# Attention weights turned by 32x32 blocks on VectorE and a DRAM scratch instead of on TensorE, in 22 of 32 attention units

## The chip, the cores and the metric

One core of a Trainium2 chip runs the whole program. The metric is device time in microseconds (us): the median of three runs of the kernel before is 690.51, with a lowest of 689.42 and a highest of 690.60. The engines are called PE (TensorE), DVE (VectorE), ACT (ScalarE), POOL (GpSimd) and SP (SyncE, which here only issues DMAs).

## What is computed

A sparse causal attention, then a two-layer block with the activation h·cos(h), all in float32 (4 batches, 8 heads, 768 positions, head size 64; 3072 tokens, model width 512, inner width 2048):

```python
scores = scale * np.matmul(q, k.transpose(0, 1, 3, 2))
keep = is_global | is_local            # first 8 keys, or the last 96 up to the query
scores = np.where(keep, scores + bias, -1000000000.0)
a = np.exp(scores - max); a = a / (sum + 1e-09)
x = np.matmul(a, v)                    # then heads side by side: tokens x 512
h = x @ w_in
out = (h * np.cos(h)) @ w_out
```

## The kernel before, in words

**Tiling.** Queries go in tiles of 96 (R). A tile sees its own 96 keys, the 96 before them and 8 global keys, so each tile keeps one row of 104 weights per query (SLOT): a column of the first 96 holds either an own key or, right of the diagonal, one of the 96 before (they never both count), and the last 8 columns are the global keys. Four tiles make a chunk of 384 tokens (8 chunks); two heads make a pair (4 pairs). A chunk and a pair make a *unit*: 32 units, numbered chunk by chunk.

**A unit** (`plan_unit`, then `plan_values`): scores on PE (L561; L557 in the first units), the fold of the two key blocks and the minimum on DVE (L574, L583), the exponential on ACT (L603), the normalization on POOL (`norm`, L631 or L626), one operation for each half of the unit (two tiles by two heads: 96 partitions x 4 x 104). Then the weights have to stand with keys on partitions: for each half `turn` (L693) does four PE transposes into a PSUM bank, and DVE writes the bank twice into the tile `pv`, through a mask, `others` (L701) for the keys of the block before and the globals, and `own` (L706) for the tile's own keys. In the leading tile of a sequence a plain copy (`whole`, L281) stands in for a mask. `av` (L728) multiplies by the values, 32 small matmuls (28 in a leading unit), and `high` (L281) and `rest` (L749) split the result into the two operands `xh`, `xl` of the next stage.

**The block.** A *step* is 128 of the 2048 inner columns for one chunk: 12 matmuls of 384 columns (`moe1`, L765), the activation on ACT and DVE (L782, L785, L788, L825), a split by `gh` (L285, L281 or L283) and `gl` (L838), and 9 matmuls of 512 columns (`moe2`, L776). There are 128 steps. `plan_store` writes finished rows out by way of the tiles `oo` (L281, L877), in two slots `wu`, in the last chunk in three slots `part`.

**The order.** A list scheduler written into the kernel (`Plan`) fixes the order of every engine before anything runs. Each operation has engines with a duration in ns, and a due time that is passed back from what needs it (`dues`); at each moment an engine takes the ready operation with the earliest due. So the engines' queues are in the order that the planner's own figures give. For an SP operation the figures are, in `run`:

```python
if e == SP:
    dma = max(end + 300, dma) + o.extra
    self.free[SP] = max(end, dma - DEPTH)
    end = dma + 1400
```

Here `end` is the issue's end (470 ns for every DMA of the kernel before), `extra` the time of the bytes, and 1400 the rest until others may go on. An operation marked `port=True` is kept from running on DVE while POOL runs, and the next POOL instruction is made to wait for it (`emit`). Buffers are slots by name: 5 of `tt` (weights, before they are turned), 3 of `pv`, 2 of `wu`, 3 of `part` (partial sums of chunk 0 while chunk 1 runs), 3 of `raw` (queries and keys as loaded), 3 PSUM banks for attention.

Of the kernel before, what the change touches and what calls it, by code (L numbers as in the profile page):

```python
# [10 lines left out]
F32 = mybir.dt.float32  # L11
# [7 lines left out]
ALU = mybir.AluOpType  # L19
PSUM = bass.MemoryType.PSUM  # L20

P = 128
# [3 lines left out]
G = 8  # L26
R = 96
SLOT = R + G
# [40 lines left out]

EXACT = 8  # L70

HOMES = 7

HOLD = 8
# [4 lines left out]
class Slot:  # L79


    def __init__(self, cls, make):
        self.cls, self.make = cls, make
        self.users = 0
        self.at = None
        self._tile = None
# [6 lines left out]


class Op:
    def __init__(self, engines, emit, after, uses, due, table, extra, port, mode):
        self.engines, self.emit, self.uses, self.due, self.table = engines, emit, uses, due, table
        self.extra, self.port, self.mode = extra, port, mode
        self.after = [a for a in after if a is not None]
        self.then = []  # L100
        self.left = len(self.after)
        self.ready = 0
        self.start = None


class Plan:
# [16 lines left out]
        self.port = self.hand = 0  # L123
        self.mode = None

    def op(self, engines, emit, after=(), uses=(), due=None, table=None, extra=0, port=False, mode=None):
        o = Op(engines, emit, after, list(uses), due, table, extra, port, mode)
        for a in o.after:
            a.then.append(o)
        for u in o.uses:  # L130
            u.users += 1
        self.ops.append(o)
        return o

    def dues(self):
        late = 10**9
        for o in reversed(self.ops):
            d = late if o.due is None else o.due
            for t in o.then:
                d = min(d, t.due - min(t.engines.values()) - self.WAIT[next(iter(o.engines))] - o.extra)  # L140
            o.due = d

    def place(self, u, t):
# [117 lines left out]
class Net:  # L261
# [376 lines left out]
    def plan_split(self, raw, src, k0, sc):  # L638
# [34 lines left out]
        k = p.op({DVE: 70 + w * 535 // 512, POOL: 100 + w * 1125 // 512}, krest, [k], [raw, kk], port=True)  # L673
        return [qq, kk], [q, k]

    def plan_values(self, u):
        nc, p, D = self.nc, self.plan, self.D
        n, pr, hs, vs, tt = u["n"], u["pr"], u["hs"], u["v"], u["tt"]
        att = "early" if n == 0 else "att"
        px = self.bank("pxearly" if n == 0 else "px")  # L680
        pvs, ready = [], list(u["lv"])
        for h in range(0, CT, 2):
            pt = self.bank(att)

            pv = Slot(self.early("pv", n, pr), lambda i: self.work.tile([P, 2, 4 * R], F32, name="pv", tag=i))
            lead = u["first"] and h == 0

            def turn(e, pt=pt, h=h, lead=lead):
                for t in range(2):
                    w = R if lead and t == 0 else SLOT  # L690
                    for j in range(2):
                        o = (2 * t + j) * R
                        nc.tensor.transpose(pt.tile[:w, o : o + R], tt[h // 2].tile[:, t, j, :w], self.ident[:R, :R])  # L693

            a = 2 if lead else 0

            wide = lambda x, a: x.rearrange("p (c i) -> p c i", i=R)[:, a:]
            mask = lambda m, a: m.rearrange("p (o i) -> p o i", o=1).broadcast_to([m.shape[0], 4 - a, R])

            def others(e, pt=pt, pv=pv, a=a):  # L700
                nc.vector.tensor_tensor(  # L701
                    wide(pv.tile[:SLOT, 0], a), wide(pt.tile[:SLOT, : 4 * R], a), mask(self.others, a), op=ALU.mult
                )

            def own(e, pt=pt, pv=pv, a=a):
                nc.vector.tensor_tensor(  # L706
                    wide(pv.tile[:R, 1], a), wide(pt.tile[:R, : 4 * R], a), mask(self.own, a), op=ALU.mult
                )

            def whole(e, pt=pt, pv=pv):  # L710
                self.copy(e, pv.tile[:R, 1, : 2 * R], pt.tile[:R, : 2 * R])

            o = self.chain("pt", p.op({PE: 340}, turn, [u["norm"][h // 2]], [pt, pv, tt[h // 2]]))
            d = 70 + (4 - a) * R * 104 // 100
            ready += [p.op({DVE: d}, fn, [o], [pt, pv]) for fn in (others, own)]
            if lead:
                ready.append(p.op({ACT: 50 + 2 * R * 427 // 512, DVE: 70 + 2 * R * 104 // 100}, whole, [o], [pt, pv]))
            pvs.append(pv)

        def av(e):  # L720
            for t in range(CT):
                pv = pvs[t // 2].tile
                lead = u["first"] and t == 0
                for c in (1,) if lead else (0, 1):
                    k = R if c else SLOT
                    for j in range(2):
                        o = (2 * (t % 2) + j) * R
                        nc.tensor.matmul(  # L728
                            px.tile[j * D : (j + 1) * D, t * R : (t + 1) * R],
                            vs.tile[:k, t + c, hs][:, j * D : (j + 1) * D],  # L730
                            pv[:k, c, o : o + R],
                            start=c == 0 or lead,
                            stop=c == 1,
                        )

        o = self.chain("av", p.op(
            {PE: 160 * (2 * CT - u["first"])}, av, ready, [px, vs] + pvs, mode="columns"))
        if n not in self.x:
            self.x[n] = Slot("x", lambda i: [
                self.work.tile([P, self.NP, CW], F32R, name=nm, tag=f"{nm}{i}") for nm in ("xh", "xl")  # L740
            ])
        x = self.x[n]

        def high(e):
            self.copy(e, x.tile[0][:, pr, :], px.tile[:, :CW])

        def rest(e):
            xh, xl = x.tile
            nc.vector.tensor_tensor(xl[:, pr, :], px.tile[:, :CW], xh.bitcast(F32)[:, pr, :], op=ALU.subtract)  # L749

        o = self.chain("xh", p.op({ACT: 370, DVE: 470}, high, [o], [px, x]))
        self.xdone[n, pr] = p.op({DVE: 470}, rest, [o], [px, x], due=self.xdue(n, pr))
# [264 lines left out]
    def run(self):  # L1017
        with ExitStack() as ctx:
            pool = lambda name, **kw: ctx.enter_context(self.tc.tile_pool(name=name, bufs=1, **kw))
            self.work, self.psum = pool("work"), pool("psum", space=PSUM)  # L1020
            with self.tc.manual_schedule():
                flag = self.windows()
        rv = self.nc.values_load(flag, min_val=0, max_val=P)
        with self.tc.If(rv > 0):
            self.general()

    def windows(self):

        NCK = self.B * self.NCH
        names = lambda nm, n: [f"{nm}{i}" for i in range(n)]  # L1030
        banks = names("b", 8)
        self.plan = Plan(
            {
                "ph": banks[0:2], "po0": banks[2:3], "po1": banks[3:4], "po2": banks[4:5], "att": banks[5:8],
                "px": banks[6:8], "early": banks[5:8] + banks[0:5], "pxearly": banks[6:8] + banks[2:5],
                "tt": names("tt", NT), "st": names("st", NST), "q": names("q", NQK), "k": names("k", NQK), "raw": names("raw", NRAW),
                "v": names("v", NV), "pv": names("pv", NPV), "ttearly": names("tt", NT) + names("k", 2),
                "vearly": names("v", NV) + ["q0"], "pvearly": names("pv", NPV) + ["q1"], "x": names("x", NX),
                "rr": names("rr", NRR), "gg": names("gg", NG), "wu": names("wu", 2), "part": names("part", NTOK),
            },  # L1040
            {PE: 400, ACT: 2400, DVE: 700, POOL: 5200, SP: 600},
        )
        self.prev, self.x, self.xdone, self.wdone, self.part = {}, {}, {}, {}, {}
        p = self.plan
        self.constants()
        self.tmp_slots = [Slot("tt", None) for _ in range(3)]
        self.plan_masks()
        phases = PHASES + [(n, 0, self.NF) for n in range(1 + max([x[0] for x in PHASES], default=-1), NCK)]
        self.seq = [(n, i, a, b - 1) for n, a, b in phases for i in range(a, b)]
        for n in range(NCK):  # L1050
            for b2 in range(self.NP // UB):
                L = self.plan_loads(n, b2)
                for i in range(UB):
                    self.plan_values(self.plan_unit(L, b2 * UB + i))
# [95 lines left out]
```

## Time and profile before

| | |
|---|---|
| timed runs | 689.42, 690.51, 690.60 us (median 690.51) |
| span of the profiled execution | 688.2 us, first to last instruction |
| its own time | not among the times shown; the timed runs lie 1.2 to 2.4 us over this span |
| PE busy | 674.0 us, 98% of the span |
| DVE, ACT, POOL busy | 417.9, 416.3, 332.7 us |
| DMA | 55.95 MB, mean 81 GB/s |
| granted TensorE clock, mean | 0.997 |

Matmuls are pipelined, so the busy time of one (246 ns for a transpose) is not what it adds to the queue; the chain of waits shows the distance from one to the next. An engine's idle time is shown with the event that ended it.

### The profile page before, as it was taken

To read this page: it belongs to the slowest core of one execution; us is meant where nothing else is said; L and a number is where in the kernel's file an instruction comes from. 1 tells how busy PE (TensorE), PEld (TensorE's weight loads), DVE (VectorE), ACT (ScalarE), POOL (GpSimd) and SP (SyncE) were. 2 spreads that over 40 slices of the span, in tenths; PEclk is the share of its full clock that TensorE was granted. 3 is DMA by queue.
4 is the path that set the end of the run, shared out by engine and by line. 5 is a ranking of instruction groups with operands and counts; after the bars stand their busy time and mean duration, and the time that the engine had idled before them with its cause. 6 is when DMAs were issued, how large, how long until landed. Compare 5 with 4: busy or idle time off the path is not lost.

```text
span 688.2 us, 12961 instructions
## 1 busy us (share of the span) xinstructions
PE 674.0 (98%) x4462; PEld 591.2 (86%) x4462; DVE 417.9 (61%) x1313; ACT 416.3 (60%) x1064; POOL 332.7 (48%) x427
## 2 busy tenths in 40 slices
PE   7999999999999999999999999999999999999995
PEld 4668899888898888888898888988889899898994
DVE  7998889976537665466736667266663566522221
ACT  6999987776546664665627666275663756423222
POOL 5777643435445553554534555345453455333332
PEclk9999999999999999999999999999999999999998
DMA  8899501142203222032322313032220310001001
GB/s 275 297 371 310 124 1 48 41 126 61 61 1 106 67 70 70 25 97 64 73 66 72 98 51 85 21 113 57 70 74 12 116 29 1 1 1 47 0 2 51
DMA packets 32603, 55.95 MB, mean 81 GB/s; under 512 B 3472, under 2 KB 18192, under 8 KB 32528
## 3 DMA queue, kind: packets, MB, share of 16 engines
q1 hardware_dynamic: 32528, 55.03, 27.2%
q8 instruction: 37, 0.61, 0.4%
q14 instruction: 38, 0.31, 0.2%
HBM read 48.73 MB, written 6.29 MB: 80 GB/s over the span
## 4 chain that ended last, share of the span: by engine, by line
PE 85%; ACT 6%; POOL 3%; DMA 2%; issue 2%; DVE 2%; SPq 0%; POOLq 0%; ACTq 0%
PE bank L776 37%; PE bank L765 36%; PE bank L728 5%; PE bank L561 5%; PE bank L693 2%; ACT tt L603 2%; DMA raw<-in_w_out_dram 1%; POOL ks L661 1%; POOL tt L631 1%; DMA out_dram<-oo 1%; DMA raw<-in_qk_dram 1%; POOL gl L838 1%; ACT L788 1%; DVE tt L583 0%; ACT w L281 0%
## 5 line engine op out<-in xcount | busy, mean ns | idle before, releaser
L765 PE MATMUL bank<-xh,w 128*128 128x384 f32 x1024 | 299.3, 342 | 1.0 <-DVE gl L838 0.8
L776 PE MATMUL bank<-w,gh 128*128 128x512 f32 x768 | 244.2, 399 | 0.0
L765 PEld LDWEIGHTS bank<-xh,w 128*128 128x128 f32 x1024 | 188.2, 188 | 9.5 <-DVE gl L838 1.8
L765 PE MATMUL bank<-xl,w 128*128 128x384 f32 x512 | 172.3, 336 | 0.0
L776 PEld LDWEIGHTS bank<-w,gh 128*128 128x128 f32 x768 | 137.9, 188 | 19.6 <-ACT tt L603 0.3
L776 PE MATMUL bank<-w,gl 128*128 128x512 f32 x384 | 151.4, 394 | 0.0
L285 POOL TENSOR_SCALAR gh<-rr 128x384 fp32r<-128x384 f32 x91 | 46.8, 514 | 210.4 <-PE bank L776 151.4
L785 DVE SCALAR_TENSOR_TENSOR rr<-rr,bank 128x384 f32<-128x384 int32 x129 | 70.5, 548 | 111.2 <-ACT rr L782 110.7
L782 ACT ACTIVATE rr<-bank 128x384 int32<-128x384 f32 x129 | 62.3, 484 | 116.4 <-PE bank L765 116.2
L788 ACT ACTIVATE rr<-rr,half_pi 128x384 f32<-128x384 f32 x129 | 79.0, 615 | 70.0 <-DVE rr L785 69.5
L765 PEld LDWEIGHTS bank<-xl,w 128*128 128x128 f32 x512 | 96.4, 188 | 4.0
L603 ACT ACTIVATE tt<-tt,worst 96x104 f32<-96x104 f32 (+1 forms) x256 | 94.4, 370 | 6.6 <-DVE worst L583 5.7
L838 POOL TENSOR_TENSOR gl<-rr,gh 128x384 fp32r<-128x384 f32 (+1 forms) x93 | 93.6, 1007 | 8.5 <-PE bank L693 1.5
L825 DVE TENSOR_TENSOR rr<-bank,rr 128x384 f32<-128x384 f32 (+1 forms) x121 | 66.2, 549 | 43.0 <-ACT rr L788 42.7
L776 PEld LDWEIGHTS bank<-w,gl 128*128 128x128 f32 x384 | 72.3, 188 | 16.7
L631 POOL TENSOR_TENSOR tt<-tt,st 96x416 f32<-96x416 f32 x48 | 42.3, 885 | 34.5 <-DVE qs L652 20.7
L583 DVE CUSTOM_DVE_ANT_0 tt<-bank,dd 96x104 f32<-96x104 f32 (+1 forms) x256 | 55.7, 257 | 2.6
L661 POOL TENSOR_TENSOR ks<-raw,ks 64x512 fp32r<-64x512 f32 (+1 forms) x39 | 47.9, 1227 | 5.4 <-POOL gl L838 2.5
L561 PEld LDWEIGHTS bank<-ks,qs 128*96 128x96 f32 x384 | 46.2, 162 | 4.6
L728 PEld LDWEIGHTS bank<-pv,v 104*64 104x64 f32 (+1 forms) x960 | 41.0, 136 | 9.2 <-issue 7.0
L561 PE MATMUL bank<-ks,qs 128*96 128x200 f32 (+1 forms) x384 | 48.2, 255 | 0.0
L603 ACT ACTIVATION_READ_ACCUMULATOR tt<-tt,worst 96x1 f32 x256 | 48.0, 188 | 0.0
(98 smaller groups left out, 730.2 us busy)
## 6 DMA issues: line engine op xcount, KB each, us to landing
raw<-in_qk_dram SPq DMA_DIRECT2D x64, 224.0 KB
raw<-in_w_out_dram SPq DMA_DIRECT2D x16, 512.0 KB
raw<-in_w_in_dram SPq DMA_DIRECT2D x16, 512.0 KB
raw<-in_qk_dram SPq DMA_DIRECT2D x32, 198.0 KB
out_dram<-oo SPq DMA_DIRECT2D x24, 256.0 KB
v<-in_v_dram SPq DMA_DIRECT2D x16, 240.0 KB
raw<-in_qk_dram SPq DMA_DIRECT2D x8, 396.0 KB
v<-in_v_dram SPq DMA_DIRECT2D x16, 192.0 KB
```

Source lines behind the costliest of these rows:

```text
L561: nc.tensor.matmul(out, qs[:, m, q0], ks[:, k : k + w], start=m == 0, stop=m == 1)
L583: nc.vector.tensor_tensor_reduce(tt[t // 2].tile[:, t % 2, j, :w], ps.tile[:R, i * WIN : i * WIN + w], self.dd[:, v, :w], op0=ALU.add, op1 ...
L603: nc.scalar.activation(x, x, AF.Exp, bias=lows[:, c : c + 1], scale=-1.0, accum_out=st.tile[:, c : c + 1])
L661: self.eng(e).tensor_tensor(ks[D:, k0:], raw.tile[D:, k0:KW], ks.bitcast(F32)[D:, k0:], op=ALU.subtract)
L728: nc.tensor.matmul(px.tile[j * D : (j + 1) * D, t * R : (t + 1) * R], vs.tile[:k, t + c, hs][:, j * D : (j + 1) * D], pv[:k, c, o : o + R] ...
L765: self.nc.tensor.matmul(ph[:, :CW], self.wi[f][:, w, kk * P : (kk + 1) * P], xx[:, kk, :], start=kk == 0 and m == 0, stop=kk == self.NK - ...
L776: self.nc.tensor.matmul(po, gg[:, ts], self.wo[f][:, w, :], start=start and m == 0, stop=stop and m == 2)
L782: self.nc.scalar.activation(r.bitcast(I32), ph, AF.Copy, scale=1.0 / TWO_PI, bias=0.25)
L785: self.nc.vector.scalar_tensor_tensor(r, r.bitcast(I32), -TWO_PI, ph, op0=ALU.mult, op1=ALU.add)
L788: self.nc.scalar.activation(r, r, AF.Sin, bias=self.half_pi)
L825: {DVE: dve}, lambda e, r=r, h=h, y=y: nc.vector.tensor_tensor(y(), h(), r(), op=ALU.mult), [o], [ph, rr]
L838: self.eng(e).tensor_tensor(g[1][:, cs], y(), g[0].bitcast(F32)[:, cs], op=ALU.subtract)
```

## The change

From unit 10 on (`TURN`), thus in 22 of the 32 units, `plan_moved` takes the place of the PE transposes. The earlier ten units keep the old way (`plan_turned`, the old code unchanged). For each half of a unit `plan_moved` does this:

- `turn` and `ends`, two DVE transposes by 32x32 blocks, out of `tt` into a tile `sw`: the first 96 columns of each row, and the last 32 columns, which hold the 8 global keys. `sw` uses the five slots `wu` and `part`.
- `store`, one DMA of `sw` (96 partitions x 2048 B) to a DRAM scratch `away` (six slots).
- three DMAs `move` back from it, each to 32 partitions in runs of 512 B, and `glob`, one for the 8 global rows; all wait for the store.
- `others` and `own` as before, but SBUF to SBUF, on POOL or DVE as the planner chooses.

`av` then reads each tile's weights as three runs of 32 columns, 128 apart. The number of matmuls in it is as before. The planner counts the landing of a DMA with 2000 ns more (`LAND`) when it passes back due times.

```diff
+TURN = 10
+LAND = 2000
+CB = R // 32
...
-                d = min(d, t.due - min(t.engines.values()) - self.WAIT[next(iter(o.engines))] - o.extra)
+                d = min(d, t.due - min(t.engines.values()) - self.WAIT[next(iter(o.engines))] - o.extra - o.land)
...
+    def plan_moved(self, u, h):
...
+        sw = Slot("sw", lambda i: self.work.tile([R, CB + 1, 4, 32], F32, name="sw", tag=i))
+        pv = Slot("pv", lambda i: self.work.tile([P, 2, 4 * R], F32, name="pv", tag=i))
+        c0 = 2 if u["first"] and h == 0 else 0
+        blocks = lambda x: x.rearrange("p (a c i) -> p a c i", c=4, i=32)
+        def turn(e):
+            x = tt[h // 2].tile.rearrange("p t j w -> p (t j) w")
+            nc.vector.transpose(sw.tile[:, :CB], x[:, :, :R].rearrange("p c (b k) -> p b c k", k=32))
+        def ends(e):
+            x = tt[h // 2].tile.rearrange("p t j w -> p (t j) w")
+            nc.vector.transpose(sw.tile[:, CB, c0:], x[:, c0:, SLOT - 32 :])
+            if c0:
+                nc.vector.transpose(sw.tile[:, CB, :c0], x[:, :c0, R - 32 : R])
+        o = self.chain("sw", p.op({DVE: 570}, turn, [u["norm"][h // 2]], [tt[h // 2], sw]))
+        q = p.op({DVE: 265}, ends, [o], [tt[h // 2], sw])
+        away = Slot("away", lambda i: self.dram.tile([R, CB + 1, 4, 32], F32, name="away", tag=i))
+        def store(e):
+            nc.sync.dma_start(away.tile, sw.tile)
+        def move(e, b):
+            nc.sync.dma_start(
+                blocks(pv.tile[32 * b : 32 * b + 32, 1]).rearrange("k a c i -> k a (c i)"),
+                away.tile[:, b].rearrange("(a k) c i -> k a (c i)", k=32),
+            )
...
+        o = self.chain("away", p.op({SP: 630}, store, [o, q], [sw, away], extra=700, land=LAND))
+        moves = [p.op({SP: 630}, lambda e, b=b: move(e, b), [o], [away, pv], extra=270, land=LAND) for b in range(CB)]
+        self.chain("moves", moves[0])
+        moves.append(p.op({SP: 630}, glob, [o], [away, pv], extra=80, land=LAND))
...
+        o = p.op({DVE: 550, POOL: 980}, others, moves, [pv], port=True)
+        o = p.op({DVE: 540, POOL: 1000}, own, [o], [pv], port=True)
+        return pv, [o]
...
+        aside = n * self.NP + pr >= TURN
...
+            pv, done = (self.plan_moved if aside else self.plan_turned)(u, h)
...
+                        if aside:
+                            w = pv[:k, c].rearrange("p (a c i) -> p a c i", c=4, i=32)[:, :, i]
...
+                "away": names("away", 6), "sw": names("wu", 2) + names("part", NTOK), "rr": names("rr", NRR), "gg": names("gg", NG), "wu": names("wu", 2), "part": names("part", NTOK),
```

## Rows read from the trace of the kernel before

**Rows 1.** The page: busy time of each engine with its share of the span and instructions, and the busy tenths (of the granted clock too) in 40 equal slices.

```profile
PE 674.0 (98%) x4462; PEld 591.2 (86%) x4462; DVE 417.9 (61%) x1313; ACT 416.3 (60%) x1064; POOL 332.7 (48%) x427
...
PE   7999999999999999999999999999999999999995
...
PEclk9999999999999999999999999999999999999998
```

**Rows 2.** The chain of waits from 145 to 600 us, shares by line.

```profile
by line: PE bank L776 37.6%; PE bank L765 37.2%; PE bank L728 7.0%; PE bank L561 6.8%; PE bank L693 3.4%; issue 2.1%; POOL ks L661 1.0%; POOL tt L631 1.0%; DMA out_dram<-oo 0.9%; POOL gl L838 0.9%; POOL ks L285 0.5%; POOL gh L285 0.5%; ACT 
```

**Rows 3.** The groups of PE instructions by line: busy us, mean ns of one, and idle time before them with what ended it.

```profile
L765 PE MATMUL bank<-xh,w 128*128 128x384 f32 x1024 | 299.3, 342 | 1.0 <-DVE gl L838 0.8
...
L728 PE MATMUL bank<-pv,v 96*64 96x96 f32 x512 | 43.3, 248 | 0.5 <-ACT pv L281 0.3 <-PE bank L557 0.2
...
L693 PE MATMUL bank<-ident,tt 96*104 96x96 f32 x224 | 29.7, 249 | 2.1 <-POOL tt L631 1.5
...
L693 PE MATMUL bank<-ident,tt 96*96 96x96 f32 x32 | 5.4, 249 | 1.4 <-POOL tt L626 1.0 <-DVE worst L583 0.4
```

**Rows 4.** The chain of waits in order of time (start us, us, what): from 302 to 316 us, and three later pieces of the value matmuls, the last ones of the run among them.

```profile
309.70 0.33 PE bank L693 x4
310.03 1.41 PE bank L776 x6
...
313.55 1.48 PE bank L728 x32
...
330.55 1.48 PE bank L728 x32
...
347.02 1.48 PE bank L728 x32
...
595.47 1.48 PE bank L728 x32
```

**Rows 5.** The timeline of one unit's end, of POOL, PE and DVE: start us, us, what, and idle time before it.

```profile
308.42 0.88 POOL L631 TENSOR_TENSOR tt<-tt,st 96x416 f32<-96x416 f32 x1 [1.32 <-DVE gl L838]
...
308.64 1.08 DVE L652 SCALAR_TENSOR_TENSOR qs<-raw,qs 128x384 fp32r<-128x384 f32 x1
...
309.80 0.88 POOL L631 TENSOR_TENSOR tt<-tt,st 96x416 f32<-96x416 f32 x1 [0.50 <-DVE qs L652]
...
312.40 0.54 DVE L706 TENSOR_TENSOR pv<-bank,own 96x384 f32<-96x384 f32 x1
...
313.48 1.55 PE L728 MATMUL bank<-pv,v 104*64 104x96 f32 x32
```

**Rows 6.** Busy time by engine from 150 to 600 us (count in brackets), granted clock, DMA share and GB/s; first all instructions, then those of L693 alone (PE, weight loads).

```profile
150.00:600.00 450.00, 449.21 (x3042) 401.31 (x3039) 262.72 (x840) 261.92 (x671) 218.31 (x268) 1.00 0.22 61
...
150.00:600.00 450.00, 21.97 (x176) 17.99 (x176) 1.00 0.22 61
```

**Rows 7.** The timelines of SP and ACT about the stores of finished rows, 256 KB each, in two slots: the third copy into `oo` waits for the landing of the first store.

```profile
373.74 0.53 SPq L877 DMA_DIRECT2D out_dram<-oo  x1
...
377.50 0.59 ACT L281 COPY oo<-bank 128x512 f32<-128x512 f32 x1 [1.03 <-DMA out_dram<-oo]
...
619.86 4.24 SPq L877 DMA_DIRECT2D out_dram<-oo  x3
...
623.16 0.58 ACT L281 COPY oo<-bank 128x512 f32<-128x512 f32 x1
...
146.43 4.29 DMA out_dram<-oo
```

**Rows 8.** What SP's DMA queue waited for from 150 to 600 us (us in total, times, longest), and the SP instructions of L645, the loads of queries and keys (duration ns min/median/max); and their commonest form in the page (times, KB each).

```profile
SPq L645 <- DVE qs L652: 246.1, 24, 23.2
SPq L466 <- PE bank L728: 53.6, 18, 4.8
...
L645 SPq DMA_DIRECT2D raw<-in_qk_dram x78: 465/556/1270, 160.2 to 557.4; - x78
...
raw<-in_qk_dram SPq DMA_DIRECT2D x64, 224.0 KB
```

**Rows 9.** Groups of DVE instructions by line, SBUF or PSUM to SBUF: busy us, mean ns of one, idle before.

```profile
L701 DVE TENSOR_TENSOR pv<-bank,others 104x384 f32<-104x384 f32 x48 | 26.5, 552 | 11.5 <-PE bank L693 11.4
L706 DVE TENSOR_TENSOR pv<-bank,own 96x384 f32<-96x384 f32 x48 | 26.1, 543 | 0.0
...
L701 DVE TENSOR_TENSOR pv<-bank,others 104x192 f32<-104x192 f32 x16 | 5.7, 354 | 2.5 <-PE bank L693 2.1 <-ACT pv L281 0.3
L706 DVE TENSOR_TENSOR pv<-bank,own 96x192 f32<-96x192 f32 x16 | 5.5, 345 | 0.8 <-ACT pv L281 0.8
...
L283 DVE CAST gh<-rr 128x384 fp32r<-128x384 f32 x6 | 2.7, 447 | 3.4 <-PE bank L776 3.4
```

**Rows 10.** POOL's groups nearest to the masks, and what POOL's normalization waited for from 150 to 600 us (us, times, longest).

```profile
L838 POOL TENSOR_TENSOR gl<-rr,gh 128x384 fp32r<-128x384 f32 x91 | 92.5, 1016 | 7.6 <-PE bank L693 1.5
...
L631 POOL TENSOR_TENSOR tt<-tt,st 96x416 f32<-96x416 f32 x48 | 42.3, 885 | 34.5 <-DVE qs L652 20.7 <-DVE gl L838 12.1 <-DVE st L614 1.7
...
POOL gh L285 <- PE bank L776: 105.3, 36, 4.6
...
POOL tt L631 <- DVE qs L652: 20.7, 18, 2.2
```

**Rows 11.** DVE operations that read two SBUF operands: L652's duration ns min/median/max, and from 150 to 600 us the busy time of L652 (DVE) and of L838 (DVE, POOL), counts in brackets.

```profile
L652 DVE SCALAR_TENSOR_TENSOR qs<-raw,qs x48: 544/559/1098, 109.2 to 575.3; 128x384 fp32r<-128x384 f32 x48
...
150.00:600.00 450.00, 29.85 (x42) 1.00 0.22 61
...
150.00:600.00 450.00, 9.66 (x16) 72.10 (x71) 1.00 0.22 61
```

More of the change, by code (lines that the diff above doesn't have):

```diff
@@ L95, with __init__ @@
 class Op:
-    def __init__(self, engines, emit, after, uses, due, table, extra, port, mode):
+    def __init__(self, engines, emit, after, uses, due, table, extra, port, mode, land):
+        self.land = land
         self.engines, self.emit, self.uses, self.due, self.table = engines, emit, uses, due, table
@@ L124, in __init__, with op @@
         self.mode = None
-    def op(self, engines, emit, after=(), uses=(), due=None, table=None, extra=0, port=False, mode=None):
-        o = Op(engines, emit, after, list(uses), due, table, extra, port, mode)
+    def op(self, engines, emit, after=(), uses=(), due=None, table=None, extra=0, port=False, mode=None, land=0):
+        o = Op(engines, emit, after, list(uses), due, table, extra, port, mode, land)
         for a in o.after:
@@ L674, in plan_split, with plan_turned, others, own @@
         return [qq, kk], [q, k]
+    def plan_turned(self, u, h):
+        nc, p = self.nc, self.plan
+        n, pr, tt = u["n"], u["pr"], u["tt"]
+        pt = self.bank("early" if n == 0 else "att")
+        pv = Slot(self.early("pv", n, pr), lambda i: self.work.tile([P, 2, 4 * R], F32, name="pv", tag=i))
+        lead = u["first"] and h == 0
+        def turn(e):
+            for t in range(2):
+                w = R if lead and t == 0 else SLOT
+                for j in range(2):
+                    o = (2 * t + j) * R
+                    nc.tensor.transpose(pt.tile[:w, o : o + R], tt[h // 2].tile[:, t, j, :w], self.ident[:R, :R])
+        a = 2 if lead else 0
+        wide = lambda x, a: x.rearrange("p (c i) -> p c i", i=R)[:, a:]
+        mask = lambda m, a: m.rearrange("p (o i) -> p o i", o=1).broadcast_to([m.shape[0], 4 - a, R])
+        def others(e):
+            nc.vector.tensor_tensor(
+                wide(pv.tile[:SLOT, 0], a), wide(pt.tile[:SLOT, : 4 * R], a), mask(self.others, a), op=ALU.mult
+            )
+        def own(e):
+            nc.vector.tensor_tensor(
+                wide(pv.tile[:R, 1], a), wide(pt.tile[:R, : 4 * R], a), mask(self.own, a), op=ALU.mult
+            )
+        def whole(e):
+            self.copy(e, pv.tile[:R, 1, : 2 * R], pt.tile[:R, : 2 * R])
+        o = self.chain("pt", p.op({PE: 340}, turn, [u["norm"][h // 2]], [pt, pv, tt[h // 2]]))
+        d = 70 + (4 - a) * R * 104 // 100
+        done = [p.op({DVE: d}, fn, [o], [pt, pv]) for fn in (others, own)]
+        if lead:
+            done.append(p.op({ACT: 50 + 2 * R * 427 // 512, DVE: 70 + 2 * R * 104 // 100}, whole, [o], [pt, pv]))
+        return pv, done
@@ new lines, in plan_moved, with turn, glob, others @@
+    def plan_moved(self, u, h):
+        nc, p = self.nc, self.plan
+        n, pr, tt = u["n"], u["pr"], u["tt"]
+        sw = Slot("sw", lambda i: self.work.tile([R, CB + 1, 4, 32], F32, name="sw", tag=i))
+        pv = Slot("pv", lambda i: self.work.tile([P, 2, 4 * R], F32, name="pv", tag=i))
+        c0 = 2 if u["first"] and h == 0 else 0
+        blocks = lambda x: x.rearrange("p (a c i) -> p a c i", c=4, i=32)
+        def turn(e):
+            x = tt[h // 2].tile.rearrange("p t j w -> p (t j) w")
[14 more added lines that the diff above has]
+                away.tile[:, b].rearrange("(a k) c i -> k a (c i)", k=32),
+            )
+        def glob(e):
+            nc.sync.dma_start(
+                blocks(pv.tile[R:SLOT, 0])[:, :, c0:].rearrange("k a c i -> k a (c i)"),
+                away.tile[:, CB, c0:].rearrange("(a k) c i -> k a (c i)", k=32)[32 - G :],
+            )
+        o = self.chain("away", p.op({SP: 630}, store, [o, q], [sw, away], extra=700, land=LAND))
+        moves = [p.op({SP: 630}, lambda e, b=b: move(e, b), [o], [away, pv], extra=270, land=LAND) for b in range(CB)]
+        self.chain("moves", moves[0])
+        moves.append(p.op({SP: 630}, glob, [o], [away, pv], extra=80, land=LAND))
+        mask = lambda m, c: m.rearrange("p (a o i) -> p a o i", o=1, i=32).broadcast_to([R, CB, 4 - c, 32])
+        def others(e):
+            self.eng(e).tensor_tensor(
+                blocks(pv.tile[:R, 0])[:, :, c0:], blocks(pv.tile[:R, 1])[:, :, c0:], mask(self.others[:R], c0),
+                op=ALU.mult,
+            )
+        def own(e):
+            x = blocks(pv.tile[:R, 1])[:, :, c0:]
+            self.eng(e).tensor_tensor(x, x, mask(self.own, c0), op=ALU.mult)
+        o = p.op({DVE: 550, POOL: 980}, others, moves, [pv], port=True)
+        o = p.op({DVE: 540, POOL: 1000}, own, [o], [pv], port=True)
+        return pv, [o]
@@ L676, in plan_values @@
     def plan_values(self, u):
         nc, p, D = self.nc, self.plan, self.D
-        n, pr, hs, vs, tt = u["n"], u["pr"], u["hs"], u["v"], u["tt"]
-        att = "early" if n == 0 else "att"
+        n, pr, hs, vs = u["n"], u["pr"], u["hs"], u["v"]
         px = self.bank("pxearly" if n == 0 else "px")
+        aside = n * self.NP + pr >= TURN
         pvs, ready = [], list(u["lv"])
         for h in range(0, CT, 2):
[L683 to L717, printed above, removed]
@@ L718, in plan_values @@
+            pv, done = (self.plan_moved if aside else self.plan_turned)(u, h)
             pvs.append(pv)
+            ready += done
         def av(e):
@@ L726, in av @@
                     for j in range(2):
-                        o = (2 * (t % 2) + j) * R
+                        i = 2 * (t % 2) + j
+                        if aside:
+                            w = pv[:k, c].rearrange("p (a c i) -> p a c i", c=4, i=32)[:, :, i]
+                        else:
+                            w = pv[:k, c, i * R : (i + 1) * R]
                         nc.tensor.matmul(
@@ L730, in av @@
                             vs.tile[:k, t + c, hs][:, j * D : (j + 1) * D],
-                            pv[:k, c, o : o + R],
+                            w,
                             start=c == 0 or lead,
@@ L1020, in run @@
             self.work, self.psum = pool("work"), pool("psum", space=PSUM)
+            self.dram = pool("dram", space=bass.MemoryType.DRAM)
             with self.tc.manual_schedule():
@@ L1038, in windows @@
                 "vearly": names("v", NV) + ["q0"], "pvearly": names("pv", NPV) + ["q1"], "x": names("x", NX),
-                "rr": names("rr", NRR), "gg": names("gg", NG), "wu": names("wu", 2), "part": names("part", NTOK),
+                "away": names("away", 6), "sw": names("wu", 2) + names("part", NTOK), "rr": names("rr", NRR), "gg": names("gg", NG), "wu": names("wu", 2), "part": names("part", NTOK),
             },
```

## The prediction

> **What bounds the kernel now.** I read first the page's busy shares and its slices: PE is busy 98% of the span and at nine tenths or more from the second slice to the last but one, at the full granted clock, while POOL has half its time free [rows 1]. Busy time of pipelined matmuls proves little, so next comes the chain of waits over 145 to 600 us, the stretch of units 10 to 31: nearly all of it is PE lines one behind the other, L693, the transposes, with 3.4% [rows 2]. The groups of PE instructions say whether PE waits: before the 1024 large matmuls 1.0 us in all, before the weights-times-values matmuls 0.5, before the transposes 2.1 + 1.4 [rows 3]. The reader is to see a queue that hardly ever waits, because its order comes from a planner whose figures fit the chip. So PE instructions on that queue are paid in full, and taking some out pays in full, as long as nothing that PE waits for becomes later than the planner thinks. All 176 transposes at stake lie between 150 and 600 us [rows 6]: 176 / 4 = 44 halves, 22 units.
>
> **What is removed from PE.** In the chain four transposes add 0.33 us between two blocks of matmuls [rows 4] (their 246 to 249 ns each [rows 3] are pipelined durations and not this distance). 44 x 0.33 = 14.5 us. The chain's share gives 3.4% of 455 us = 15.5 us [rows 2]; it holds also the starts where the transposes came just after the normalization. I take 15.5, with 14.5 as the other end. The end of the kernel feels it, since from 150 us on PE is busy 449.2 of 450 us [rows 6] and no later stage waits for anything but PE.
>
> **What moves to DVE.** Removed are two masks from PSUM per half, 0.552 + 0.543 us, in the six leading halves 0.354 + 0.345 [rows 9]: 38 x 1.095 + 6 x 0.70 = 45.8 us. A DVE transpose stands in no row. By the nearest, 384 columns cost 0.45 (a cast) to 0.55 us and 192 columns 0.35 [rows 9]; the slope of the masks, about 0.2 us for 192 columns, puts the 128 columns of `ends` at 0.29. With a blocked operation as upper end, 1.10 us [rows 11], a half costs 0.74 to 1.4 us; I take 0.55 + 0.29 = 0.84, as the masks are the nearest rows: 44 x 0.84 = 37 us, 9 less than before. DVE has 187 of the 450 us free [rows 6], so this hides in any case.
>
> **The masks, now SBUF to SBUF.** On POOL one costs between 0.885 us (96 partitions, 416 columns) and 1.016 us (128 partitions, 384) [rows 10]; I take 0.95. 76 full ones and 12 half ones at 0.5: 72 + 6 = 78 us, if all go there. POOL goes from 218 to 296 of 450 us [rows 6]. It spends 105 us waiting for PE to release a buffer before `gh` [rows 10], and that idle time is what hides the masks; without it each would push a `gl`.
>
> **The trip through DRAM.** Per half a store of 192 KB, three loads of 48 KB and one of 12 KB: 0.36 MB, 15.7 MB in all, 35 GB/s on top of 61 at a DMA share of 0.22 [rows 6]. Bandwidth is no limit. SP issues 220 more DMAs; an issue took 0.47 to 0.56 us as a rule [rows 8], so 5 x 0.56 x 2 = 5.6 us per unit, and units follow each other by 16.5 us or more (330.55 to 347.02) [rows 4]. SP's queue spends 246 us waiting for a `raw` buffer and 54 for the values' [rows 8], and the new issues lie there. Behind a `move` that waits for the store's landing stand the next unit's loads of queries, keys and values; ACT and POOL, which take them, waited for no such load in this stretch, so a few us cost nothing.
>
> What counts is latency. Before, the second normalization ends at 310.68 and the value matmuls start at 313.48 [rows 5]: 2.8 us. After, the same path is 0.84 (DVE) + 3.3 (store) + 4.4 (loads) + 1.9 (two masks) = 10.4 us. The 7.6 us more need not cost PE anything: the planner knows of them and puts steps of the block in front. But PE's order is fixed, and the planner takes the value matmuls as soon as by its figures they are ready (before, they started 0.54 us after the last mask, 312.40 + 0.54 to 313.48 [rows 5]). So what PE pays is the difference between the chip and the figures. The store by the figures: 630 + 300 + 700 + 1400 = 3.03 us. The chip: stores of 256 KB released their slot 3.30 us after issue at the latest when alone (619.86 to 623.16), 3.76 beside loads (373.74 to 377.50), 4.29 behind loads [rows 7]. That is up to 1.26 us more. The four loads by the figures: 4 x 630 + 300 + 80 + 1400 = 4.3 us; on the chip three issues at 0.56 and then the last one's landing, at least its 0.56 with the planner's 1.7 and at most the 3.30 of a far larger store: 3.9 to 5.0 us. Together -0.4 to 2.0 us late per unit. From that goes half a PE block of 0.53 or 0.70 us, some 0.3, since the planner too waits for a block to end. A gain below zero is excluded, as PE would simply be on time: 0 to 1.7 us per unit, 0 to 37 us over 22. I take 0.25 us, nearer the lone store than the crowded one, because the queue is idle for most of a unit: 22 x 0.25 = 5.5 us.
>
> The Trainium skill ("DMA: Bandwidth & Descriptors", section "Anatomy of one DMA — SWDGE (gpsimd) path") gives a DMA a fixed 2.0 us plus its bytes at 436 GB/s, most of it the write's receipt, longest towards HBM; its section is about POOL's path, not SP's. By it the store would land in an estimated 2.45 us, before the planner expects it, and the sum would be 690.5 - 15.5 = 675; by the same rule a 256 KB store takes 2.6 us, and the trace has up to 3.30, so I go by the trace.
>
> **Reading the weights in runs of 32.** `av` keeps its 32 matmuls of 96 columns, 1.48 us in the chain [rows 4]. No row has such runs in fp32; between 0 and a tenth of 22 x 1.48 = 32.6 us, 3.3. I take 0. The PSUM banks of the transposes come free, which can only help scores.
>
> **Sum.** -15.5 + 5.5 = -10.0 us. The profiled span is 688.2, the median 2.3 above it, and the difference is set against the median: 680.5 us. A measurement of this kernel can tell about 0.2%, 1.4 us, from no change.
>
> **Rivals.**
> *The landing comes late (slower).* PE stands at the value matmuls until the second half's masks are written. Its place is L728 after the change, its price the lateness times 22, and it decides from 15.5 / 22 = 0.70 us per unit on. With the crowded store (+1.26) and loads 0.1 over, less 0.3, it is 1.06 us: 690.5 - 15.5 + 23.3 = 698. For it: every store that shared the queue with loads was 0.7 to 1.3 us over the figure [rows 7], and each unit loads 0.9 MB of queries and keys in four DMAs [rows 8]. Against it: an issue at 630 is generous beside 556 [rows 8].
> *POOL and DVE shut each other out (about no change).* L652, with two SBUF operands, took 1.08 us instead of 0.54 when a normalization ran on POOL (308.42 to 309.30) [rows 5, 11], and the normalization waited 20.7 us for such operations [rows 10]. The new masks read two SBUF operands on either engine and are the last link before PE. If each meets half of such an operation, 2 x 0.27 x 22 = 12 us come on top: 692. Against it: the planner already keeps the two apart, and there is room on average: 296 us of POOL and 29.9 + 9.7 = 40 of such DVE work in 450 [rows 11]. The Trainium skill ("SBUF — State Buffer", section "Who interferes with whom") says it as a rule, a DVE instruction with two SBUF inputs and a POOL instruction that reads SBUF exclude each other for a whole instruction; the 1.08 us agree.
>
> **The numbers.** The forecast, a gain of 3 to 16 us, has 0.58; its own range is 674 to 687. The late landing has 0.25, of which 0.24 slower and 0.01 the same. The shut-out has 0.17, of which 0.10 still faster and 0.07 the same. Faster 0.68, same 0.08, slower 0.24. The lower end is the whole of the transposes and the last of their waits, 674; the upper end reaches into the late landing, to about 0.85 us per unit (690.5 - 15.5 + 18.7 = 694), and leaves some 15% above it, 4% below.
>
> **What would show it.** Right: 80 transposes left on PE; DVE transposes of about 0.55 and 0.29 us; the chain still PE lines; idle before the value matmuls under 6 us in all; the block's matmuls at unchanged distances; the last value matmuls some 10 us sooner than 595.5 [rows 4]. Wrong: PE idle of 15 us or more before the value matmuls, ended by a mask on POOL or DVE that itself followed a DMA (late landing) or an operation of the other engine (shut-out); or PE waiting at a `moe2` for a `gl` behind masks. Masks mostly on DVE would move 50 us there and change nothing for PE.

## The result and the profile after

The changed kernel takes 672.87 us (672.85 to 672.97) against 690.56 of the kernel before: a ratio of 0.9748, 95% interval 0.9734 to 0.9762, 17.7 us less. The forecast was 680.5 with 674 to 694: the direction was right, the gain was larger than forecast by 7.6 us, and the time lies 1.1 us below the range. The profiled span went from 688.2 to 671.2 us, 17.0 less; the other 0.7 lies outside the spans.

The page, as in [rows 1] (busy time, share, instructions; then the tenths in 40 slices):

```profile
span 671.2 us, 13136 instructions
...
PE 656.6 (98%) x4286; PEld 577.4 (86%) x4286; DVE 423.7 (63%) x1360; ACT 426.0 (63%) x1084; POOL 362.0 (54%) x446
...
PE   7999999999999999999999999999999999999995
...
PEclk9999999999999999999999999999999999999998
DMA  8899601044415433354314444144442511000001
```

PE is as full as before in a shorter span, with 176 instructions fewer; POOL has 29 us more, and DMA, mostly at 2 to 3 tenths before in the middle of the run, is now mostly at 3 to 5. The chain of waits from 145 to 585 us answers to [rows 2]:

```profile
by line: PE bank L841 42.8%; PE bank L852 41.2%; PE bank L804 7.2%; PE bank L566 7.0%; DVE tt L588 0.3%; DVE rr L861 0.2%; DVE pv L708 0.2%; DVE bank L579 0.2%; DVE pv L703 0.2%; DVE rr L901 0.1%; DVE xl L825 0.1%; DVE sw L733 0.1%; DVE xh 
```

No DMA and no mask of the new way stands in it; the new transposes (L733) hold 0.1%. L841 and L852 are the old L765 and L776, L804 is the value matmuls and L566 the scores; the four make up 98% where they made up 89%. PE's groups with their idle time, as in [rows 3]:

```profile
L841 PE MATMUL bank<-xh,w 128*128 128x384 f32 x1024 | 294.7, 340 | 1.7 <-DVE rr L901 0.9 <-DVE gl L914 0.8
...
L804 PE MATMUL bank<-pv,v 96*64 96x96 f32 x512 | 43.4, 248 | 0.5 <-ACT pv L286 0.3 <-PE bank L562 0.2
...
L695 PE MATMUL bank<-ident,tt 96*104 96x96 f32 x60 | 8.7, 253 | 1.5 <-POOL tt L636 1.3
```

The value matmuls wait 0.5 us in all, as before: the late landing that the prediction charged with 5.5 us is not there. After 145 us there is one new wait, before a block matmul:

```profile
151.49 0.40 PE L852 MATMUL bank<-w,gl 128*128 128x512 f32 x1
152.78 0.45 PE L841 MATMUL bank<-xh,w 128*128 128x384 f32 x1 [0.89 <-DVE rr L901]
...
150.23 1.28 ACT L864 ACT_TABLE_LOAD   x1
151.52 0.61 ACT L864 ACTIVATE rr<-rr,half_pi 128x384 f32<-128x384 f32 x1
...
151.96 0.20 DVE L739 STREAM_TRANSPOSE sw<-tt 96x64 f32<-96x64 f32 x1
152.17 0.56 DVE L901 TENSOR_TENSOR rr<-bank,rr 128x384 f32<-128x384 f32 x1
```

From 151.49 to 152.78 are 1.29 us where 0.23 is usual, so 1.06 us are lost there. The operation that PE waits for (L901) stands behind the first moved unit's transposes on DVE, which end at 152.16; but what it needs from ACT (L864) is done only at 152.13, behind a table load of 1.28 us. So the transposes alone do not explain this wait. What the new operations cost (DVE and POOL groups; busy us, mean ns):

```profile
L733 DVE STREAM_TRANSPOSE sw<-tt 96x384 f32<-96x384 f32 x44 | 24.8, 563 | 6.6 <-POOL tt L636 5.2 <-POOL tt L631 0.7 <-DMA out_dram<-oo 0.4
L775 DVE TENSOR_TENSOR pv<-pv,own 96x384 f32<-96x384 f32 x22 | 11.7, 547 | 0.1
L737 DVE STREAM_TRANSPOSE sw<-tt 96x128 f32<-96x128 f32 x38 | 10.2, 269 | 0.0
...
L768 POOL TENSOR_TENSOR pv<-pv,others 96x384 f32<-96x384 f32 x31 | 31.5, 1017 | 2.9 <-DMA pv<-away 2.3
```

The reader is to see 0.56 and 0.27 us for the DVE transposes (0.55 and 0.29 were predicted) and 1.02 for a mask on POOL (0.95). Now the way through DRAM. The fence shows the timeline of SP early, when it issues nothing else in between, and then SP, POOL and PE at a later unit:

```profile
163.72 0.34 SPq L747 DMA_DIRECT2D away<-sw  x1
165.81 1.69 SPq L750 DMA_DIRECT2D pv<-away  x3
...
330.10 1.69 SPq L650 DMA_DIRECT2D raw<-in_qk_dram  x2
331.89 0.53 SPq L747 DMA_DIRECT2D away<-sw  x1
...
336.54 1.25 SPq L750 DMA_DIRECT2D pv<-away  x3
337.83 0.33 SPq L756 DMA_DIRECT2D pv<-away  x1
338.27 1.25 SPq L750 DMA_DIRECT2D pv<-away  x3
339.56 0.33 SPq L756 DMA_DIRECT2D pv<-away  x1
...
339.50 1.01 POOL L768 TENSOR_TENSOR pv<-pv,others 96x384 f32<-96x384 f32 x1 [0.55 <-DMA pv<-away]
340.59 1.01 POOL L775 TENSOR_TENSOR pv<-pv,own 96x384 f32<-96x384 f32 x1
341.56 1.02 POOL L768 TENSOR_TENSOR pv<-pv,others 96x384 f32<-96x384 f32 x1
342.53 1.01 POOL L914 TENSOR_TENSOR gl<-rr,gh 128x384 fp32r<-128x384 f32 x1
343.50 1.03 POOL L775 TENSOR_TENSOR pv<-pv,own 96x384 f32<-96x384 f32 x1
...
345.75 1.47 PE L804 MATMUL bank<-pv,v 104*64 104x96 f32 x30
```

The store issued at 163.72 has landed by 165.81, when the first load is issued: 2.09 us, where the planner has 3.03. The last load of a half, issued at 337.83, has landed by 339.50, when a mask that waited for it starts: 1.67 us; with the 1.29 us between the first load's issue and the last one's (336.54 to 337.83) the four take 2.96, where the planner has 4.3. So here the chip is 0.94 + 1.34 = 2.3 us ahead of the planner's figures. This holds for a store that has the queue to itself: behind two loads of queries and keys, in the later unit, the first load goes out 4.65 us after the store (331.89 to 336.54). The planner's `dma` counts such a queue too, so this is not all lateness. The second half's masks do not wait for a DMA but stand in POOL's queue, and PE takes the value matmuls 1.2 us after the last of them (343.50 + 1.03 to 345.75); over the 22 units this distance is 0.24 to 1.68 us by the timeline.

### The profile page after: what moved, and what is told of

It reads as the page before. It is cut to its first block, busy times and chain, and to the rows that moved or that the text cites. A ratio compares the mean times of both kernels' runs of the same rounds, so it can differ in the third digit from the quotient of the medians.

```text
span 671.2 us, 13136 instructions
## 1 busy us (share of the span) xinstructions
PE 656.6 (98%) x4286; PEld 577.4 (86%) x4286; DVE 423.7 (63%) x1360; ACT 426.0 (63%) x1084; POOL 362.0 (54%) x446
## 4 chain that ended last, share of the span: by engine, by line
PE 88%; ACT 7%; DVE 2%; DMA 1%; issue 0%; SPq 0%; POOL 0%; POOLq 0%; ACTq 0%
PE bank L852 39%; PE bank L841 39%; PE bank L804 5%; PE bank L566 5%; ACT tt L608 3%; DMA raw<-in_qk_dram 1%; ACT raw L411 1%; ACT L864 1%; DVE tt L588 1%; ACT w L286 1%; ACT raw L427 0%; DVE bank L579 0%; ACT L608 0%; ACT raw L525 0%; ACT rr L864 0%
## 5 line engine op out<-in xcount | busy, mean ns | idle before, releaser
L841 PE MATMUL bank<-xh,w 128*128 128x384 f32 x1024 | 294.7, 340 | 1.7 <-DVE rr L901 0.9
L852 PE MATMUL bank<-w,gh 128*128 128x512 f32 x768 | 242.0, 397 | 0.0
L841 PEld LDWEIGHTS bank<-xh,w 128*128 128x128 f32 x1024 | 187.8, 188 | 10.4 <-DVE rr L901 2.0
L841 PE MATMUL bank<-xl,w 128*128 128x384 f32 x512 | 172.1, 336 | 0.0
L852 PEld LDWEIGHTS bank<-w,gh 128*128 128x128 f32 x768 | 139.7, 188 | 22.2 <-ACT oo L286 0.8
L852 PE MATMUL bank<-w,gl 128*128 128x512 f32 x384 | 151.5, 394 | 0.0
L864 ACT ACTIVATE rr<-rr,half_pi 128x384 f32<-128x384 f32 x129 | 78.7, 614 | 48.5 <-DVE rr L861 47.9
L841 PEld LDWEIGHTS bank<-xl,w 128*128 128x128 f32 x512 | 96.4, 188 | 4.0
L290 POOL TENSOR_SCALAR gh<-rr 128x384 fp32r<-128x384 f32 x67 | 34.3, 512 | 118.2 <-PE bank L852 99.9
L901 DVE TENSOR_TENSOR rr<-bank,rr 128x384 f32<-128x384 f32 (+1 forms) x121 | 65.7, 545 | 46.8 <-ACT rr L864 46.5
L852 PEld LDWEIGHTS bank<-w,gl 128*128 128x128 f32 x384 | 72.3, 188 | 16.4
L636 POOL TENSOR_TENSOR tt<-tt,st 96x416 f32<-96x416 f32 x48 | 44.6, 937 | 43.7 <-DVE qs L657 21.4
L804 PEld LDWEIGHTS bank<-pv,v 104*64 104x64 f32 (+1 forms) x960 | 41.1, 136 | 10.2 <-issue 6.4
L566 PEld LDWEIGHTS bank<-ks,qs 128*96 128x96 f32 x384 | 45.9, 162 | 4.5
L566 PE MATMUL bank<-ks,qs 128*96 128x200 f32 (+1 forms) x384 | 47.8, 254 | 0.0
L804 PE MATMUL bank<-pv,v 104*64 104x96 f32 (+1 forms) x960 | 47.0, 248 | 0.5 <-ACT pv L286 0.3
```

The source lines that it names most:

```text
L566: nc.tensor.matmul(out, qs[:, m, q0], ks[:, k : k + w], start=m == 0, stop=m == 1)
L636: self.eng(e).tensor_tensor(x, x, r.broadcast_to([R, 4, SLOT]), op=ALU.mult)
L804: nc.tensor.matmul(px.tile[j * D : (j + 1) * D, t * R : (t + 1) * R], vs.tile[:k, t + c, hs][:, j * D : (j + 1) * D], w, start=c == 0 or lead,
L841: self.nc.tensor.matmul(ph[:, :CW], self.wi[f][:, w, kk * P : (kk + 1) * P], xx[:, kk, :], start=kk == 0 and m == 0, stop=kk == self.NK - ...
L852: self.nc.tensor.matmul(po, gg[:, ts], self.wo[f][:, w, :], start=start and m == 0, stop=stop and m == 2)
L864: self.nc.scalar.activation(r, r, AF.Sin, bias=self.half_pi)
```

## The experiments

Times are medians, each beside runs of the kernel before on the same chip (690.1 to 690.6; 689.9 for the last two runs). Q stands for the theory that PE's queue alone counts, T for a cost of the way through DRAM, O for another order as the source.

**What the transposes cost PE.** First they are put back beside the new way, with nobody reading what they write:

```diff
...
+        self.chain("pt", p.op({PE: 340}, again, [u["norm"][h // 2]], [pt, tt[h // 2]]))
         o = self.chain("sw", p.op({DVE: 570}, turn, [u["norm"][h // 2]], [tt[h // 2], sw]))
```

> The changed kernel with the PE transposes of units 10 to 31 left in beside the new way (44 groups of four, into a PSUM bank that nothing reads). Theory Q (all that counts is PE's queue: a group of transposes costs it about 0.36 us with the matmul behind it, and the way through DRAM costs nothing): 672.9 + 44 x 0.36 = 688.7, between 687 and 691. Theory T (the way through DRAM costs PE the 5.5 us of the prediction, so that the transposes were worth 23): 696. Theory O (half of the gain comes from another order that the planner found, not from the transposes): 680 or less.

782.08 us: a miss of the experiment, and no verdict. As nothing waited for these transposes they had no due time, and the planner left them for last: some stand over 100 us behind the DVE transposes of the same half, and they hold the buffers of weights meanwhile. So again with a due time:

```diff
+        back = self.chain("pt", p.op({PE: 340}, again, [u["norm"][h // 2]], [pt, tt[h // 2]]))
...
-        return pv, [o]
+        return pv, [o, back]
```

> As the run before with the PE transposes left in beside the new way, but with a due time: the value matmuls count as waiting for them, so that the planner no longer leaves them to the end while they hold the weight buffers. Theory Q (PE's queue alone): 672.9 + 44 x 0.36 = 688.7, between 687 and 691. Theory O (another order): 684 or less.

687.67 us (686.83 to 688.83), 14.8 more than the changed kernel: Q is within its bounds, and O, which wanted 684 or less, falls. And the kernel before with each transpose twice:

```diff
-                        nc.tensor.transpose(pt.tile[:w, o : o + R], ...)
+                        for _ in range(2 if n * self.NP + pr >= 10 else 1):
+                            nc.tensor.transpose(pt.tile[:w, o : o + R], ...)
-            o = self.chain("pt", p.op({PE: 340}, turn, ...
+            o = self.chain("pt", p.op({PE: 680 if n * self.NP + pr >= 10 else 340}, turn, ...
```

> The kernel before with each of the 176 transposes of units 10 to 31 issued twice in a row (44 groups of eight), the planner told 680 ns in place of 340. Every matmul more at its distance in the queue, 0.083 us: 690.3 + 176 x 0.083 = 704.9. If a transpose costs by its share of the whole gain, 17.7 / 176 = 0.10: 708. The difference of the two, 3 us, is what a group costs on top by its place (the matmul behind it and the wait ahead of it).

708.86 us, 18.3 more than before. By the time this agrees with 0.10 us each, but not for that reason: PE's waits show new ones in this run, for queries and keys:

```profile
PE bank L561 <- DVE qs L652: 2.4, 1, 2.4
...
PE bank L561 <- POOL ks L661: 0.8, 1, 0.8
```

14.6 us of matmuls and 3.2 of these waits make 17.8, and behind the longer wait the granted clock stood at its lower level for 3.4 us (158.5 to 161.9), so the run does not tell the two prices apart. The price is better read from the timeline of PE in the kernel before, by starts:

```profile
291.31 0.34 PE L765 MATMUL bank<-xh,w 128*128 128x384 f32 x1
291.80 0.54 PE L693 MATMUL bank<-ident,tt 96*104 96x96 f32 x4
292.12 0.42 PE L765 MATMUL bank<-xh,w 128*128 128x384 f32 x1
292.38 0.34 PE L765 MATMUL bank<-xl,w 128*128 128x384 f32 x1
292.55 0.34 PE L765 MATMUL bank<-xh,w 128*128 128x384 f32 x1
292.73 0.49 PE L693 MATMUL bank<-ident,tt 96*104 96x96 f32 x4
293.01 0.71 PE L776 MATMUL bank<-w,gh 128*128 128x512 f32 x2
293.56 0.39 PE L776 MATMUL bank<-w,gl 128*128 128x512 f32 x1
```

A matmul of L765 usually lies 0.174 us from the next, one of L776 0.233. The second group: from 292.55 to 293.56 are 1.01, less 0.174 and 2 x 0.233 leaves 0.37. The first group came too early for its weights: from 291.31 to 292.38 are 1.07, less 2 x 0.174 leaves 0.72. The same working over the starts of the 44 groups of units 10 to 31 gives a median of 0.362 and a mean of 0.403 us. So the 44 groups cost 17.7 us before: 44 x 0.362 = 15.9 for the transposes with the delay of the matmul behind them, and 1.8 of lateness in six groups, most of it ahead of them. By the same working the 44 groups that were put back cost 15.9 us in all. In that run two of the groups stand where the new wait was, and 0.40 us of it are left (PE waits there 0.23 us, until 152.54, for the same DVE operation); these 0.40 are in the 15.9. Putting back thus gives 15.9 less the 1.06 us of the new wait: 14.8, as measured.

**Whether the way through DRAM costs anything.** This kernel leaves out the DVE transposes, the store and the loads, and the masks read the weights as they stand, so that its output is another:

```diff
...
-        o = p.op({DVE: 550, POOL: 980}, others, moves, [pv], port=True)
+        done.append(p.op({DVE: 550, POOL: 980}, others, norm, [tt[h // 2], pv], port=True))
...
```

> The changed kernel without the DVE transposes, the store and the loads: the masks read the weights as they stand, the 8 global rows are set to zero, so the weights are not turned and the output is another. Theory Q: the way through DRAM is hidden, 672.9 within 1.5. Theory T: 667.4, shorter by the 5.5 us that the way costs.

678.04 us: slower by 5.2 than with the way, which neither theory expected. The waits of PE:

```profile
PE bank L817 <- DVE rr L877: 2.3, 8, 0.4
...
PE bank L828 <- ACT oo L286: 1.2, 1, 1.2
```

With the weights ready sooner the planner makes another order, in which PE waits eight times for a block's DVE work and once for a store's copy; by the starts of its matmuls these nine places lose 5.0 us. Without them it would stand at 673, where T wants 667.4. T falls, as far as one run with another order can say. Next the planner's figure, the work unchanged:

```diff
-                        end = dma + 1400
+                        end = dma + 1400 - (1000 if o.land else 0)
```

> The changed kernel, but the planner believes that every DMA of the way through DRAM lands 1.0 us sooner (two in a row: 2.0 us per unit). The work is unchanged, only the order is more hopeful. If the landing is what ends last before the masks and the planner's margin covered it (rival of the late landing, with the figures as cover): PE waits before the value matmuls, 22 x (2.0 - 0.9) = 24 us, 697. If the masks are held by their engines and the margin is wide: under 3 us, 673 to 676.

673.54 us (672.81 to 674.29): no change beyond 1.5. Taking 2.0 us from the figures leaves them about as the chip is (2.03 for the store against 2.09), so it takes the margin and no more. Then the way itself longer, by one and by two copies:

```diff
-            nc.sync.dma_start(away.tile, sw.tile)
...
+            nc.sync.dma_start(far[0], sw.tile)
+            for x, y in zip(far, far[1:] + [None]):
+                nc.sync.dma_start(away.tile if y is None else y, x)
```

> The changed kernel with one more copy, DRAM to DRAM, between the store and the loads of every half, of which the planner knows nothing: the weights come some 2.1 to 2.5 us later than without it. The planner's figures have about 0.94 us to spare for the store (3.03 against 2.09 measured after the change) and 1.3 for the loads (4.3 against 1.29 + 1.67). Rival of the late landing, with 2.2 us as the point from which it decides: 0 to 0.3 us per unit, 673 to 680. If there were no margin: 22 x 2.3 = 50 us more, 723.

> As before with two more copies, some 4.2 to 5.0 us later. Rival of the late landing beyond its point: 22 x (4.6 - 2.2 - 0.5) = 42 us more, 700 to 730. If the way through DRAM is off PE's path for another reason than the planner's margin (buffers, engines of the masks): 673 to 680.

736.98 and 856.88 us. Both expectations missed the size: they counted one delay per unit, and no clock. A copy waits on SP for the store, and the other half's store stands behind it, so that a unit pays twice. What SP waited for and PE's group of the value matmuls with one copy, the wait that the second copy adds, and the heads of the two pages:

```profile
SPq L752 <- DMA far<-sw: 118.2, 44, 4.3
```

```profile
L809 PE MATMUL bank<-pv,v 104*64 104x96 f32 (+1 forms) x960 | 58.3, 266 | 24.9 <-POOL pv L780 10.9 <-POOL pv L773 10.7 <-DVE pv L780 1.2
```

```profile
SPq L752 <- DMA far<-far: 93.8, 44, 2.3
...
span 735.9 us, 13203 instructions
...
PE 687.7 (93%) x4286; PEld 596.0 (81%) x4286; DVE 430.1 (58%) x1360; ACT 426.2 (58%) x1084; POOL 362.7 (49%) x446
...
span 853.4 us, 13287 instructions
...
PE 729.9 (86%) x4286; PEld 629.3 (74%) x4286; DVE 428.5 (50%) x1360; ACT 427.7 (50%) x1084; POOL 361.6 (42%) x446
```

118.2 / 44 = 2.7 us per copy, 5.4 per unit. The time added (64.1 us, then 119.9) is not all waiting: the same 4286 matmuls keep PE busy 31.1 us longer with one copy and 42.2 more with two, at mean granted clocks of 0.965 and 0.889 against 0.997. PE's idle time (span less busy) grows by 33.6 us with the first copy, 24.4 of them before the value matmuls, and by 75.3 with the second. Per unit 1.5 of 5.4 us reach PE as idle time with the first copy, and 3.4 of 93.8 / 22 = 4.3 with the second. So the rival of the late landing is real, once a reserve is used up. Its size does not come out of these two runs: the first copy leaves about 4 us unpaid, more than the 2.3 read from the landings, and the run with the planner's figures lowered shows only that 2.0 are there.

**How many units.** `TURN` = 21, 8 and 4 in place of 10.

> The change for the last 11 units only. Theory Q: each unit is worth 17.7 / 22 = 0.80 us, so 672.9 + 11 x 0.80 = 681.7, between 680.5 and 683. Theory O (order): no reason for a straight line; 676 or 688 as well.

> The change from unit 8 on instead of 10, so 24 units. Theory Q: 2 x 0.77 us less (the price that 11 units showed): 671.3, if the two slots that are free before chunk 0 is finished and the traffic of the weights leave the planner's margin of some 2.5 us per unit whole. If not: above 672.9.

> The change from unit 4 on, 28 units. Theory Q alone: 672.9 - 6 x 0.77 = 668.3. But units 4 to 7 stand in the first 100 us, where the DMA engines are busy with the weights and the slots of the DVE tile hold weights; there PE waits anyway: slower than the change, 673 to 690, if the landing is late.

681.37, 681.46 and 691.53 us. Eleven units give 8.7 (against 690.1 beside them) and twenty-two 17.7: 0.8 us per unit both times, as by the groups (17.7 / 22). Units 8 and 9 cost 8.6 instead of giving 1.5, and units 4 to 9 lose the whole gain, which is more than was expected. With eight as first unit PE waits four times for DVE work (2.2 us at 119, 0.8 at 136, 1.3 and 1.4 at 148 to 151 us), and its granted clock falls twice (one of the two stretches is in the last section). With four, idle matmuls, which the kernel puts in where the planner expects PE to wait in the first 100 us, take most of the loss; first with four, then with ten:

```profile
L1158 PE MATMUL idle<-zeros 128*128 128x512 bf16 x112 | 28.9, 403 | 1.1 <-DVE zeros L296 1.1
...
L1158 PE MATMUL idle<-zeros 128*128 128x512 bf16 x44 | 13.6, 437 | 1.1 <-DVE zeros L296 1.1
```

So the planner itself expects PE to wait longer there when these units are moved.

**Where the masks run.** All on POOL, or all on DVE (`{POOL: 980}` and `{POOL: 1000}`, or `{DVE: 550}` and `{DVE: 540}`).

> The changed kernel with both masks of every moved half on POOL (31 of the 88 move there from DVE). POOL gets 31 x 1.02 = 32 us more of 450. Rival of the shut-out: later masks, up to 22 x 0.5 = 11 us more, 684. If PE has the margin of some 2.5 us per unit: 672.9 within 1.5.

> The changed kernel with both masks of every moved half on DVE (57 of the 88 move there from POOL). DVE gets 57 x 0.55 = 31 us more of 450 and the masks get shorter by 0.5 us each. Rival of the shut-out: each holds POOL back, up to 11 us more, 684. If there is margin: 672.9 within 1.5.

676.93 and 672.83 us. On DVE nothing changes; on POOL 4.1 us are lost, more than the 1.5 that a margin of PE would leave and a third of what the shut-out was charged with, mostly by PE waiting at block matmuls and scores (3.2 us more there by the starts) and not at the value matmuls. No version beat the change by more than its interval.

**PE's waits ahead of the transposes alone.** `POOL: 1150` for `POOL: 850` in the normalization:

> The kernel before, with the planner told 1150 ns in place of 850 for a normalization on POOL (measured: 885 on average, up to 1194), so that the transposes stand later in PE's queue and no longer wait for it. Nothing else changes. If PE's waits ahead of the transposes are a part of the gain: 1.6 us of idle time in units 10 to 31 go, 689.0 (688 to 689.6). If the rest lies in the order otherwise: 690.6.

> The changed kernel with the same figure. It has only the transposes of the first ten units left on PE, and the one wait of 1.06 us at 151 us, which another order may take away or not: 671.8 to 673.

697.11 and 684.13 us, misses: the figure also moves the first ten units, whose order is fragile (in the first run PE stands 1.9 us for `rr` at 160 us). The 1.8 us thus rest on the starts of PE's rows, not on a run.

## Why the prediction was wrong

- *What bounds the kernel, what pays.* Right: PE's queue; 0.8 us per unit, in a straight line.
- *Removed from PE: 15.5.* Too small: 17.7. [Rows 4] give 0.33 for a group, but the next matmul is late by a further 0.03, and six groups lost 1.8 us more. [Rows 3] do not show it: of the 3.5 us of idle time before 64 groups all but 0.6 lie before 150 us, in units that keep the old way. Only the distances of the starts do, and I did not take them; the chain's share follows the longest way and credits such waits to POOL. The transposes at stake, in the kernel before, from 150 us on (12 more of another shape have no idle time):

```profile
L693 PE MATMUL bank<-ident,tt 96*104 96x96 f32 x164 | 21.0, 247 | 0.6 <-POOL tt L631 0.2
```

- *Added wait: 22 x 0.25 = 5.5.* **This is the step that failed**: PE waits nothing more at the value matmuls, 5.5 of the 7.6 us by which the forecast missed; most of the rest is the term above. I priced the store from [rows 7], where the next event after a landing, a copy that had its own queue, was taken as the landing: 3.30 us as upper end became nearly my value, and 2.09 was the chip's with the queue empty. I took SP's issue at 0.56 where these loads came 0.43 apart as a rule, and so I had the chip behind the planner's figures by 0.25 us per unit, where it was 2.3 ahead of them. The Trainium skill ("DMA: Bandwidth & Descriptors", section "Anatomy of one DMA — SWDGE (gpsimd) path") gives 2.0 us plus bytes for POOL's path, an estimated 2.45 for the store; this lies 0.4 over the 2.09 measured on SP's and nearer than my row.
- *The sum.* 17.7 - 1.06 (one new wait, not foreseen) = 16.6 of the 17.0 us of the spans; 0.4 and the 0.7 outside the spans stay without a cause.
- *DVE, POOL, the masks, strided reads.* Sizes right within a tenth, but for the half masks on POOL (0.60 us for 0.5); all hidden, with 31 masks on DVE and 57 on POOL. The value matmuls still take 1.48 us in the chain.
- *The shut-out.* Not in the change itself, where no mask took over 1.03 us on POOL or 0.56 on DVE; with all masks on POOL a third of its price is lost, but whether by the shut-out is not shown.
- *The last value matmuls* came at 581.25, 14 us sooner than in [rows 4] (10 predicted):

```profile
581.25 1.48 PE bank L804 x32
```

## What to carry to other kernels

On a full engine the price of a piece of work is the distance it puts between its neighbours' starts, the neighbour behind it included; add the waits ahead of it. A long way around costs nothing while the figures that made the fixed order lie above the chip's, and it is paid once that reserve is used up: find the reserve before pricing the lateness, and take landings from a waiter that had nothing else to do. Moving a piece off the full engine can lose in a stage where that engine then has to wait for the others, as in units 4 to 9 here.

## What the runs showed of the hardware beyond that

A wait of PE can cost more than its length. With eight as first unit, PE stood 2.23 us before 121.19; the windows (PE, PEld, DVE, ACT, POOL busy, then granted clock, DMA share, GB/s) then show:

```profile
114.00:118.00 4.00, 4.00 (x19) 3.12 (x18) 3.97 (x10) 4.00 (x15) 1.44 (x3) 1.00 0.13 40
...
121.50:125.40 3.90, 3.90 (x15) 3.90 (x14) 2.73 (x4) 1.36 (x4) 3.24 (x4) 0.56 0.39 103
125.60:129.00 3.40, 3.40 (x22) 3.26 (x21) 1.72 (x8) 2.15 (x4) 2.98 (x3) 1.00 0.49 135
```

After the wait the granted clock fell to 0.56 on average, mostly the lower level of 1.2 GHz, with 15 matmuls in 3.9 us against 22 in 3.4 afterwards. The changed kernel's wait of 0.89 us at 152.8 had no such stretch behind it. The kernel with one copy more, where PE waits often, has a mean clock of 0.965 against 0.997, so part of its 64 us is this.
